# Attention and two MLPs on one core: the first attention unit worked in halves of three chunks

## Chip, cores and metric

The kernel runs on one core of one Trainium2 chip. The metric is the device time of one execution in microseconds (us).

## What is computed

Three stages follow one another. A gated linear attention makes `x`; a mixture of eight experts routes its 3072 rows by capacity and puts each through one expert; a gated MLP with RMS norm makes the output. The change touches the attention alone:

```python
B, H, S, D = q.shape                      # 4, 8, 768, 48
f = 1.0 / (1.0 + np.exp(-f_logit))
for t in range(S):
    state = f[:, :, t, :, None] * state + np.einsum('bhd,bhe->bhde', k[:, :, t], v[:, :, t])
    y[:, :, t] = np.einsum('bhd,bhde->bhe', q[:, :, t], state)
```

## The kernel before

**Attention** (`attention`, lines 323 to 539). The 32 heads are worked in 16 units of two heads, each head's 48 values of `d` on partitions 0 to 47 or 64 to 111, time along the free axis. A unit's 768 steps are six chunks of 128. One unit goes through these steps:

- `load` (line 348): SP's queue brings `f`, `k`, `q` (128x768, 384 KB each, laid out so on the host) and `v` (288 KB). There are three buffers of `f`, `k`, `q` and four of `v`; from unit 3 on each of the first comes as two transfers of 48 rows.
- `decays` (394): ACT makes `G`, the sigmoid of `f`, and `fs`, its first column of each chunk.
- `scans` (401): VectorE sets six columns of `G` (405), makes the running product `P` of the decays in each chunk by one scan over all 768 columns (406), takes six reciprocals (408), makes the inverse products `W` by a second scan from the back (409), and `kt` = k times W (418). GpSimd makes `qt` = q times P in two halves of 384 columns (414) and `e` (416).
- `k_back` (425): TensorE transposes five chunks of `kt`, three into one bank of PSUM and two into another, and ACT copies them to `kn` (432).
- `inner` (434): TensorE's products `kt` by `qt`, six chunks for two heads, in two groups of three chunks with a bank for each head (443); ACT copies a bank to `at` (449) and GpSimd masks it (450). The text calls these copies and masks.
- `sums` (452): TensorE's ten products `kn` by `v` into `U` (457), then VectorE's scan `st` over the chunks (461).
- `ends` (420): ACT keeps the last column of each chunk (`pall`) and `z`.
- `values` (464), two units later: TensorE makes `y` from `st`, `qt`, `at`, `v` (475), and ACT copies it to `YT` (481). After every fourth unit come the router's logits (`logits`, `logits_sum`).

The order is written out by hand: the scheduler is off, each engine has its instructions in the order of the program, and a unit `i` of the loop at line 509 issues `values(i-2)`, `k_back(i)`, `scans(i+1)`, `inner(i)`, `decays(i+2)`, `sums(i)`, `ends(i+1)`, then the loads of `f`, `k`, `q` for unit `i+4`:

```python
    for i in range(-1, NU + 2):
        ...
        if on(i):
            k_back(i)
        ...
        if on(i + 1):
            scans(i + 1)
        if i < 0:
            ends(0)
        if on(i):
            inner(i)
```

So unit 0 is scanned in the round `i = -1`, and its TensorE work lies in round 0, behind the instructions of unit 1's scans on VectorE and GpSimd. `bank()` hands out four banks of PSUM in turn. Ahead of the loop TensorE multiplies `ident` by itself eight times (502), without use of the result; this is called warm-up here. Two small loads are issued on ACT's queue ahead of the first sigmoid: `gcol` (720, the norm's weights, used in the last stage) and `wgp` (377, in two parts, the router's weights, used by the logits). A transfer signals one of eight completion counters; they are handed out in turn over SP's and ACT's transfers, and a transfer's issue waits until the one that had its counter before has landed.

**Behind attention.** The routing, then the experts and the gated MLP, are not touched.

Of the kernel before, what the change touches and what calls it, by code (L numbers as in the profile page):

```python
# [7 lines left out]
F32 = mybir.dt.float32  # L8
# [5 lines left out]
OP = mybir.AluOpType  # L14
# [308 lines left out]
def attention(tc, fT, kT, qT, vL, YT, w_gate, lg, pmin, ident, extra):  # L323
# [23 lines left out]
    def raw(nm, i):  # L347
        return RAW[nm, i % NR]
# [15 lines left out]
    load("fkq", 0)  # L364
# [11 lines left out]
    for h in range(2):  # L376
        nc.scalar.dma_start(wgp[64 * h:64 * h + D, :, 0:8], w_gate.rearrange("(p h d) e -> h d p e", h=2, d=D)[h])
# [15 lines left out]
    def decays(i):  # L393
        if not 0 <= i < NU:
            return
        G[i] = wk.tile([128, S + 1], F32, name="G")
        FS[i] = wk.tile([128, NC], F32, name="fs")
        nc.scalar.activation(G[i][:, 0:S], raw("f", i), AF.Sigmoid)
        nc.scalar.activation(FS[i], raw("f", i)[:, 0:S:C], AF.Sigmoid)

# [19 lines left out]
    def ends(i):  # L420
        if on(i):
            nc.scalar.copy(pall[:, i], P[i][:, C - 1:S:C])
            nc.scalar.copy(Z[i % 2][:, :, 1:], EZ[i][:, None, :].to_broadcast([128, D, NC - 1]))

    def k_back(i):
        KN[i] = wk.tile([128, NC, 128], F32, name="kn")
        for g, m in ((0, 3), (1, 2)):
            o = bank().rearrange("p (n c) -> p n c", n=3)
            for n in range(m):
                c0 = (3 * g + n) * C  # L430
                nc.tensor.transpose(o[:, n, :], KT[i][:, c0:c0 + C], ident)
            nc.scalar.copy(KN[i][:, 3 * g:3 * g + m], o[:, 0:m])

    def inner(i):

        AT[i] = wk.tile([128, 2, NC, C], F32, name="at", bufs=3)
        for g in range(2):
# [63 lines left out]
    for _ in range(8):  # L501
        nc.tensor.matmul(o, ident, ident, start=True, stop=True)
    decays(0)
    load("q", 1)
# [3 lines left out]
    for i in range(-1, NU + 2):  # L508
# [7 lines left out]
        if on(i):  # L516
            k_back(i)
        if i == NU - 1:
            extra["range"]()
        if on(i + 1):  # L520
            scans(i + 1)
        if i < 0:
            ends(0)
        if on(i):
            inner(i)
            decays(i + 2)
            sums(i)
            ends(i + 1)
# [161 lines left out]
def tile_kernel(ctx, tc, q, k, v, f_logit, w_gate, w1, w2, w2_gate, w2_val, w2_out, rms_g, fT, kT, qT, vL, out):  # L690
# [29 lines left out]
    nc.scalar.dma_start(gcol, rms_g.rearrange("(c p) -> p c", p=128))  # L720
# [21 lines left out]
    attention(tc, fT, kT, qT, vL, YT, w_gate, lg, pmin, ident,  # L742
# [460 lines left out]
```

## Time and profile before

| what | value |
|---|---|
| median of 3 runs | 836.42 us (835.05 to 838.92) |
| the profiled execution | 838.31 us, its span 836.6 us |
| TensorE busy | 804.6 us, 96% of the span |
| VectorE, ACT, GpSimd busy | 58%, 47%, 33% |
| mean granted clock of TensorE | 0.983 |
| warm-up products | 1.55 to 5.33 us |
| attention's sixteenth unit, first transposes | 105.56 us |

The span runs from the first to the last instruction. "Granted clock" is the share of TensorE's full clock that it was given: 1.00 is 2.4 GHz, 0.50 is 1.2 GHz. A row of the timeline gives the start, the time, the engine and line, what was written from what, and how many instructions were merged; in square brackets stands how long the engine was idle before it and what ended that. A 128x128 product in float32 shows as two instructions, a transpose as one. ACTq and SPq are the issue of transfers, not the transfers.

### The profile page before, as it was taken

How to read it: one execution, taken by the hardware profiler on the slowest of the kernel's cores; microseconds unless marked ns; L12 is line 12 of the kernel's file. 1: busy time of each engine (PE TensorE's matmuls, PEld its weight loads, DVE VectorE, ACT ScalarE, POOL GpSimd, SP SyncE). 2: the span in 40 equal slices, each digit the busy share in tenths (PEclk: the TensorE clock that was granted, in tenths of full speed). 3: DMA queues.
4: the chain of work that ended last, by engine and by line, in shares of the span. 5: the costliest groups of instructions: out<-in, count | busy, mean ns of one | idle time of the engine just before them, and what ended most of it. 6: DMA issues, size and time to landing. Idle time of an engine off the chain costs nothing.

```text
span 836.6 us, 16614 instructions
## 1 busy us (share of the span) xinstructions
PE 804.6 (96%) x6609; PEld 775.5 (93%) x6609; DVE 484.0 (58%) x868; ACT 392.0 (47%) x833; POOL 274.3 (33%) x327
## 2 busy tenths in 40 slices
PE   6999997899999999999999999999999999999996
PEld 5878876799999899999999999999999999999996
DVE  7988858488888888674443434344344434344332
ACT  5877636155555554576343443424243443424221
POOL 7877700348777677350112020110102020110100
PEclk8999998799999999999999999999999999999998
DMA  9986228487886697541000000000000000000000
GB/s 275 227 214 182 58 69 298 136 294 240 304 266 230 233 316 270 183 151 39 1 20 20 2 20 1 20 2 20 1 20 21 1 20 1 20 1 20 2 20 19
DMA packets 43684, 88.55 MB, mean 106 GB/s; under 512 B 5424, under 2 KB 22832, under 8 KB 43600
## 3 DMA queue, kind: packets, MB, share of 16 engines
q1 hardware_dynamic: 34528, 70.89, 27.0%
q0 software_dynamic: 3072, 9.44, 3.3%
q10 hardware_dynamic: 6000, 7.09, 2.4%
q8 instruction: 53, 0.87, 0.4%
q14 instruction: 31, 0.25, 0.1%
HBM read 70.89 MB, written 16.52 MB: 104 GB/s over the span
## 4 chain that ended last, share of the span: by engine, by line
PE 61%; issue 8%; DVE 8%; DMA 2%; ACT 2%; POOL 1%; ACTq 0%; DVEq 0%; POOLq 0%
PE o L572 5%; PE o L570 5%; PE o L571 5%; PE g L570 5%; PE g L572 5%; PE g L571 5%; PE v L572 5%; PE v L570 5%; PE v L571 5%; PE x L571 3%; PE x L572 2%; PE x L570 2%; DVE w L762 2%; PE h L571 2%; PE h L570 2%
## 5 line engine op out<-in xcount | busy, mean ns | idle before, releaser
L1127 DVE TENSOR_TENSOR hf<-sg,v 128x256 f32<-128x256 f32 x144 | 59.9, 416 | 165.3 <-PE v L572 115.1
L893 POOL TENSOR_TENSOR xlo<-xn,xhi 128x256 fp32r<-128x256 f32 x36 | 29.5, 823 | 312.2 <-ACT xhi L892 312.2
L1130 ACT CAST hh<-hf 128x256 fp32r<-128x256 f32 x144 | 58.6, 407 | 132.7 <-DVE hf L1127 132.7
L572 PE MATMUL g<-xhi,w 128*128 128x256 f32 x432 | 119.3, 276 | 0.0
L571 PE MATMUL g<-xlo,w 128*128 128x256 f32 x432 | 119.2, 276 | 0.0
L572 PE MATMUL v<-xhi,w 128*128 128x256 f32 x432 | 119.2, 276 | 0.0
L570 PE MATMUL v<-xhi,w 128*128 128x256 f32 x432 | 119.2, 276 | 0.0
L571 PE MATMUL v<-xlo,w 128*128 128x256 f32 x432 | 119.2, 276 | 0.0
L570 PE MATMUL g<-xhi,w 128*128 128x256 f32 x432 | 119.2, 276 | 0.0
L1131 DVE TENSOR_TENSOR hl<-hf,hh 128x256 fp32r<-128x256 f32 x144 | 61.3, 425 | 68.1 <-ACT hh L1130 68.1
L572 PE MATMUL o<-w,hl 128*128 128x384 f32 x288 | 98.6, 342 | 0.0
L570 PE MATMUL o<-w,hh 128*128 128x384 f32 x288 | 97.6, 339 | 0.2 <-ACT hh L1130 0.2
L571 PE MATMUL o<-w,hh 128*128 128x384 f32 x288 | 97.1, 337 | 0.0
L1125 ACT ACTIVATE sg<-g 128x256 f32<-128x256 f32 x144 | 55.3, 384 | 87.9 <-PE g L572 87.4
L570 PEld LDWEIGHTS g<-xhi,w 128*128 128x128 f32 x432 | 81.1, 188 | 0.0
L572 PEld LDWEIGHTS g<-xhi,w 128*128 128x128 f32 x432 | 81.1, 188 | 0.0
L570 PEld LDWEIGHTS v<-xhi,w 128*128 128x128 f32 x432 | 81.1, 188 | 0.0
L571 PEld LDWEIGHTS v<-xlo,w 128*128 128x128 f32 x432 | 81.1, 188 | 0.0
L572 PEld LDWEIGHTS v<-xhi,w 128*128 128x128 f32 x432 | 81.1, 188 | 0.0
L571 PEld LDWEIGHTS g<-xlo,w 128*128 128x128 f32 x432 | 81.0, 188 | 0.0
L958 POOL TENSOR_TENSOR nr<-nr,ne 128x384 f32<-128x384 f32 x36 | 61.4, 1707 | 45.7 <-DVE ne L957 12.5
L571 PE MATMUL x<-hl,w 128*128 128x384 f32 x192 | 65.6, 342 | 5.0 <-DVE hl L1032 4.8
(222 smaller groups left out, 1890.2 us busy)
## 6 DMA issues: line engine op xcount, KB each, us to landing
wraw<-in_moe_w_dram SPq DMA_DIRECT2D x32, 768.0 KB, 6.3
v<-in_v_rows_dram SPq DMA_DIRECT2D x16, 288.0 KB, 4.9
x_dram<-xrows SPq DMA_DIRECT2D x24, 192.0 KB, 4.8
nraw<-in_moe_w_gate_dram SPq DMA_DIRECT2D x12, 384.0 KB, 4.3
nraw<-in_moe_w_val_dram SPq DMA_DIRECT2D x12, 384.0 KB, 4.2
nraw<-in_moe_w_out_dram SPq DMA_DIRECT2D x12, 384.0 KB, 3.5
raw_f<-in_f_logit_turned_dram SPq DMA_DIRECT2D x26, 144.0 KB, 5.5
raw_k<-in_k_turned_dram SPq DMA_DIRECT2D x26, 144.0 KB, 5.0
```

Of the source, the lines that this page charges most:

```text
L570: nc.tensor.matmul(out, lhs[0], rhs[0], start=first, stop=False)
L571: nc.tensor.matmul(out, lhs[0], rhs[1], start=False, stop=False)
L572: nc.tensor.matmul(out, lhs[1], rhs[0], start=False, stop=last)
L762: eng.tensor_tensor(out=lo, in0=raw, in1=hi.bitcast(F32), op=OP.subtract)
L893: eng.tensor_tensor(out=lo, in0=s, in1=hi.bitcast(F32), op=OP.subtract)
L958: nc.gpsimd.tensor_tensor(out=r, in0=r, in1=e2.bitcast(F32), op=OP.mult)
L1125: nc.scalar.activation(sg, pg, AF.Silu)
L1127: nc.vector.tensor_tensor(out=h, in0=sg, in1=pv, op=OP.mult)
L1130: nc.scalar.copy(hh, h)
L1131: nc.vector.tensor_tensor(out=hl, in0=h, in1=hh.bitcast(F32), op=OP.subtract)
```

## The change

Unit 0 is worked in halves of three chunks (384 columns). Its `f` comes in two transfers; ACT's sigmoid is two instructions; VectorE does memset, scan, reciprocal, scan and `kt` for the first half and then for the second (`scans_half`). TensorE transposes and multiplies the first half (`k_back(0, (0,))`, `inner(0, (0,))`), then the second. All of this is now issued in round -1, ahead of unit 1's scans, with `ends(0)` behind it. The warm-up has 13 products instead of 8. The loads of `wgp` and `gcol` are issued behind the first sigmoids.

```diff
@@ -361,7 +361,10 @@
-    load("fkq", 0)
+    HF = (slice(0, S // 2), slice(S // 2, S))
+    for t in HF:
+        nc.sync.dma_start(raw("f", 0)[:, t], fT[0][:, t])
+    load("kq", 0)
     load("fk", 1)
...
@@ -373,8 +376,6 @@
-    for h in range(2):
-        nc.scalar.dma_start(wgp[64 * h:64 * h + D, :, 0:8], w_gate.rearrange("(p h d) e -> h d p e", h=2, d=D)[h])
...
@@ -395,8 +396,26 @@
-        nc.scalar.activation(G[i][:, 0:S], raw("f", i), AF.Sigmoid)
+        for t in HF if i == 0 else (slice(0, S),):
+            nc.scalar.activation(G[i][:, t], raw("f", i)[:, t], AF.Sigmoid)
         nc.scalar.activation(FS[i], raw("f", i)[:, 0:S:C], AF.Sigmoid)
+
+    def scans_half(t):
+        g, a, b = G[0], t.start, t.stop
+        if a == 0:
+            P[0], W[0], KT[0] = (wk.tile([128, S], F32, name=n) for n in ("P", "W", "kt"))
+            QT[0] = wk.tile([128, S], F32, name="qt", bufs=3)
+        nc.vector.memset(g[:, a + (C if a else 0):b:C], BIG * 1.0e8)
+        nc.vector.tensor_tensor_scan(out=P[0][:, t], data0=g[:, t], data1=one[:, t], initial=1.0, op0=OP.mult,
+                                     op1=OP.min)
+        nc.vector.reciprocal(g[:, a + C:b + 1:C], P[0][:, a + C - 1:b:C])
+        nc.vector.tensor_tensor_scan(out=W[0][:, t][:, ::-1], data0=g[:, b:a:-1], data1=one[:, t], initial=1.0,
+                                     op0=OP.mult, op1=OP.max)
+        nc.gpsimd.tensor_tensor(out=QT[0][:, t], in0=raw("q", 0)[:, t], in1=P[0][:, t], op=OP.mult)
+        if a:
+            EZ[0] = wk.tile([128, NC - 1], F32, name="e")
+            nc.gpsimd.tensor_tensor(out=EZ[0], in0=P[0][:, C - 1:S:C][:, 0:NC - 1], in1=FS[0][:, 1:], op=OP.mult)
+        nc.vector.tensor_tensor(out=KT[0][:, t], in0=raw("k", 0)[:, t], in1=W[0][:, t], op=OP.mult)
...
@@ -422,19 +441,22 @@
-    def k_back(i):
-        KN[i] = wk.tile([128, NC, 128], F32, name="kn")
-        for g, m in ((0, 3), (1, 2)):
+    def k_back(i, gs=(0, 1)):
+        if 0 in gs:
+            KN[i] = wk.tile([128, NC, 128], F32, name="kn")
+        for g in gs:
+            m = 3 - g
...
-    def inner(i):
+    def inner(i, gs=(0, 1)):
...
@@ -498,9 +520,12 @@
-    for _ in range(8):
+    for _ in range(13):
         nc.tensor.matmul(o, ident, ident, start=True, stop=True)
     decays(0)
+    for h in range(2):
+        nc.scalar.dma_start(wgp[64 * h:64 * h + D, :, 0:8], w_gate.rearrange("(p h d) e -> h d p e", h=2, d=D)[h])
+    nc.scalar.dma_start(gcol, rms_g.rearrange("(c p) -> p c", p=128))
     load("q", 1)
...
@@ -513,16 +538,22 @@
-        if on(i):
+        if i > 0 and on(i):
             k_back(i)
         if i == NU - 1:
             extra["range"]()
-        if on(i + 1):
+        if i < 0:
+            for t in HF:
+                scans_half(t)
+            for g in range(2):
+                k_back(0, (g,))
+                inner(0, (g,))
+            ends(0)
+        elif on(i + 1):
             scans(i + 1)
-        if i < 0:
-            ends(0)
         if on(i):
-            inner(i)
+            if i:
+                inner(i)
...
@@ -717,7 +748,6 @@
-    nc.scalar.dma_start(gcol, rms_g.rearrange("(c p) -> p c", p=128))
```

The orders that result, for the places that the prediction speaks of. `bank` and `U` are in PSUM; numbers behind `raw_` and `v_` tell buffers apart. First TensorE from its first instruction to unit 1's sums, before:

```order
L502 MATMUL bank<-ident 128x128 x8
L431 MATMUL bank<-ident,kt 128x128 x5
L443 MATMUL bank<-qt,kt 128x128 x12
L457 MATMUL U<-v_113,kn 48x48 x10
L431 MATMUL bank<-ident,kt 128x128 x5
L443 MATMUL bank<-qt,kt 128x128 x12
L457 MATMUL U<-v_114,kn 48x48 x10
```
and in the changed kernel:

```order
L524 MATMUL bank<-ident 128x128 x13
L452 MATMUL bank<-ident,kt 128x128 x3
L465 MATMUL bank<-qt,kt 128x128 x6
L452 MATMUL bank<-ident,kt 128x128 x2
L465 MATMUL bank<-qt,kt 128x128 x6
L479 MATMUL U<-v_112,kn 48x48 x10
L452 MATMUL bank<-ident,kt 128x128 x5
L465 MATMUL bank<-qt,kt 128x128 x12
L479 MATMUL U<-v_113,kn 48x48 x10
```
The six products of the first half now stand ahead of the second half's two transposes. GpSimd from its last constant on, before:

```order
L62 IOTA pid 128x1
L414 TENSOR_TENSOR qt<-raw_q_110,P 128x384 x2
L416 TENSOR_TENSOR e<-P,fs 128x5
L414 TENSOR_TENSOR qt<-raw_q_111,P 128x384 x2
L416 TENSOR_TENSOR e<-P,fs 128x5
L450 AFFINE_SELECT at<-at 128x384 x4
L414 TENSOR_TENSOR qt<-raw_q_112,P 128x384 x2
```
and now:

```order
L62 IOTA pid 128x1
L414 TENSOR_TENSOR qt<-raw_q_109,P 128x384 x2
L417 TENSOR_TENSOR e<-P,fs 128x5
L472 AFFINE_SELECT at<-at 128x384 x4
L433 TENSOR_TENSOR qt<-raw_q_110,P 128x384 x2
L435 TENSOR_TENSOR e<-P,fs 128x5
L433 TENSOR_TENSOR qt<-raw_q_111,P 128x384 x2
```
Unit 0's four masks moved from behind unit 1's `qt` to ahead of it. ACT from its first instruction on, before:

```order
L720 DMA gcol<-in_moe_rms_g_dram 128x3x1
L377 DMA wgp<-in_moe_w_gate_dram 48x4x8 x2
L398 ACT_TABLE_LOAD
L398 ACTIVATE G<-raw_f_104 128x768
L399 ACTIVATE fs<-raw_f_104 128x6
L398 ACTIVATE G<-raw_f_105 128x768
L399 ACTIVATE fs<-raw_f_105 128x6
L422 COPY pall<-P 128x6
L423 COPY z_137<-e 128x48x5
L432 COPY kn<-bank 128x384
L432 COPY kn<-bank 128x256
```
and now:

```order
L400 ACT_TABLE_LOAD
L400 ACTIVATE G<-raw_f_103 128x384 x2
L401 ACTIVATE fs<-raw_f_103 128x6
L527 DMA wgp<-in_moe_w_gate_dram 48x4x8 x2
L528 DMA gcol<-in_moe_rms_g_dram 128x3x1
L400 ACTIVATE G<-raw_f_104 128x768
L401 ACTIVATE fs<-raw_f_104 128x6
L453 COPY kn<-bank 128x384
L471 COPY at<-bank 128x384 x2
L453 COPY kn<-bank 128x256
L471 COPY at<-bank 128x384 x2
L441 COPY pall<-P 128x6
```
The table load comes first, the small loads stand between the sigmoids of units 0 and 1, and unit 0's copies stand ahead of `pall` and `z`. SP's queue from its fifth transfer on, with what each issue waits for (DMAHW0 to DMAHW7 are the completion counters), before:

```order
L359 DMA raw_k_108<-in_k_turned_dram 128x768
L359 DMA raw_q_111<-in_q_turned_dram 128x768 [waits DMAHW0_49]
L355 DMA v_113<-in_v_rows_dram 128x576 [waits DMAHW1_49]
L359 DMA raw_f_106<-in_f_logit_turned_dram 128x768 [waits DMAHW2_49]
L359 DMA raw_k_109<-in_k_turned_dram 128x768 [waits DMAHW3_49]
L359 DMA raw_q_112<-in_q_turned_dram 128x768 [waits DMAHW4_49]
L355 DMA v_114<-in_v_rows_dram 128x576 [waits DMAHW5_49]
L362 DMA raw_f_104<-in_f_logit_turned_dram 48x768 [waits DMAHW6_49,Activation_49]
```
and now:

```order
L359 DMA raw_k_107<-in_k_turned_dram 128x768
L359 DMA raw_q_110<-in_q_turned_dram 128x768 [waits DMAHW1_49]
L355 DMA v_112<-in_v_rows_dram 128x576 [waits DMAHW2_49]
L359 DMA raw_f_105<-in_f_logit_turned_dram 128x768 [waits DMAHW3_49]
L359 DMA raw_k_108<-in_k_turned_dram 128x768 [waits DMAHW4_49]
L359 DMA raw_q_111<-in_q_turned_dram 128x768 [waits DMAHW5_49]
L355 DMA v_113<-in_v_rows_dram 128x576 [waits DMAHW6_49]
L362 DMA raw_f_103<-in_f_logit_turned_dram 48x768 [waits DMAHW7_49,DMAHW0_49,Activation_49]
```
In the changed kernel the counters 5, 7 and 0 are those of `wgp` and `gcol`, so the third `q` and the fourth `f` wait for these.

## Rows read from the trace of the kernel before

**Rows 1.** Timeline of TensorE: start us, us, engine line op, tile, count.

```profile
22.12 0.77 PE L431 MATMUL bank<-ident,kt 128*128 128x128 f32 x5
...
22.82 1.68 PE L443 MATMUL bank<-qt,kt 48*128 48x128 f32 x24
...
25.01 1.42 PE L475 MATMUL yp<-qt,st 48*48 48x128 f32 x20
...
27.81 0.77 PE L431 MATMUL bank<-ident,kt 128*128 128x128 f32 x5
...
105.56 0.77 PE L431 MATMUL bank<-ident,kt 128*128 128x128 f32 x5
```

**Rows 2.** Same view, the first 17 us.

```profile
1.55 3.78 PE L502 MATMUL bank<-ident 128*128 128x128 f32 x16 [1.55 <-POOL ident L710]
...
10.60 1.33 PE L431 MATMUL bank<-ident,kt 128*128 128x128 f32 x5 [5.27 <-DVE G L405]
...
15.70 1.00 PE L431 MATMUL bank<-ident,kt 128*128 128x128 f32 x5
...
16.63 1.92 PE L443 MATMUL bank<-qt,kt 48*128 48x128 f32 x24
```

**Rows 3.** Timeline of VectorE, units 0 to 3.

```profile
5.34 0.06 DVE L405 MEMSET G<- 128x6 f32 x1 [1.86 <-ACT G L398]
...
9.24 1.31 DVE L418 TENSOR_TENSOR kt<-raw_k,W 128x768 f32<-128x768 f32 x1
...
10.50 0.06 DVE L405 MEMSET G<- 128x6 f32 x1
...
14.41 0.96 DVE L418 TENSOR_TENSOR kt<-raw_k,W 128x768 f32<-128x768 f32 x1
...
15.88 0.76 DVE L461 TENSOR_TENSOR_SCAN st<-U,z 128x288 f32<-128x288 f32 x1 [0.51 <-PE U L457]
...
16.77 1.75 DVE L406 TENSOR_TENSOR_SCAN P<-G,one 128x768 f32<-128x768 f32 x1
...
22.33 1.75 DVE L406 TENSOR_TENSOR_SCAN P<-G,one 128x768 f32<-128x768 f32 x1
```

**Rows 4.** Windows: us, busy by engine, PEclk (granted clock), DMA share, GB/s.

```profile
9.00:9.50 0.50, 0.00 (x0) 0.00 (x0) 0.47 (x2) 0.50 (x2) 0.50 (x1) 0.90 1.01 387
16.00:16.50 0.50, 0.50 (x5) 0.46 (x3) 0.50 (x1) 0.50 (x3) 0.50 (x2) 0.78 1.12 240
```

**Rows 5.** Timeline of SP's queue, ACT and GpSimd, the first 14 us.

```profile
0.82 0.40 SPq L359 DMA_DIRECT2D raw_f<-in_f_logit_turned_dram  x1
...
2.39 1.28 ACT L398 ACT_TABLE_LOAD   x1 [2.39 <-DVE wgp L375]
...
4.42 0.84 ACT L398 ACTIVATE G<-raw_f 128x768 f32<-128x768 f32 x1 [0.75 <-DMA raw_f<-in_f_logit_turned_dram]
...
7.79 1.95 POOL L414 TENSOR_TENSOR qt<-raw_q,P 128x384 f32<-128x384 f32 x2 [1.46 <-DMA raw_q<-in_q_turned_dram]
...
8.66 0.84 ACT L398 ACTIVATE G<-raw_f 128x768 f32<-128x768 f32 x1 [3.29 <-DMA raw_f<-in_f_logit_turned_dram]
...
12.44 1.96 POOL L414 TENSOR_TENSOR qt<-raw_q,P 128x384 f32<-128x384 f32 x2 [1.83 <-DVE P L406]
```

**Rows 6.** Windows of the first loads (columns as in rows 4).

```profile
2.00:3.00 1.00, 1.00 (x7) 1.00 (x7) 0.81 (x5) 0.61 (x1) 1.00 (x2) 1.00 0.95 270
3.00:4.00 1.00, 1.00 (x6) 1.00 (x6) 0.28 (x2) 0.67 (x1) 0.79 (x5) 1.00 0.69 124
```

**Rows 7.** Line 450 (masks): duration ns min/median/max, first and last start us.

```profile
L450 POOL TENSOR_SCALAR_AFFINE_SELECT at<-at x1: 1247/1247/1247, 14.5 to 14.5; 128x384 f32<-128x384 f32 x1
...
L450 POOL TENSOR_SCALAR_AFFINE_SELECT at<-at x2: 520/521/522, 16.2 to 16.7; 128x384 f32<-128x384 f32 x2
```

**Rows 8.** Timeline of SP's queue and ACT: f of unit 3.

```profile
9.41 0.83 SPq L362 DMA_DIRECT2D raw_f<-in_f_logit_turned_dram  x2
...
19.12 0.86 ACT L398 ACTIVATE G<-raw_f 128x768 f32<-128x768 f32 x1
```

More of the change, by code (lines that the diff above doesn't have):

```diff
@@ L320, in slots, with attention @@
         nc.vector.tensor_copy(ix[:, :, 2:3], t1[:, :, 2:3])
-def attention(tc, fT, kT, qT, vL, YT, w_gate, lg, pmin, ident, extra):
+def attention(tc, fT, kT, qT, vL, YT, w_gate, lg, pmin, ident, gcol, rms_g, extra):
     nc = tc.nc
@@ L432, in k_back @@
             nc.scalar.copy(KN[i][:, 3 * g:3 * g + m], o[:, 0:m])
-    def inner(i):
-        AT[i] = wk.tile([128, 2, NC, C], F32, name="at", bufs=3)
-        for g in range(2):
+    def inner(i, gs=(0, 1)):
+        if 0 in gs:
+            AT[i] = wk.tile([128, 2, NC, C], F32, name="at", bufs=3)
+        for g in gs:
             o = [bank().rearrange("p (n c) -> p n c", n=3) for _ in range(2)]
@@ L741, in tile_kernel @@
     ctx.enter_context(tc.manual_schedule())
-    attention(tc, fT, kT, qT, vL, YT, w_gate, lg, pmin, ident,
+    attention(tc, fT, kT, qT, vL, YT, w_gate, lg, pmin, ident, gcol, rms_g,
               {-2: consts, 1: lambda bank: turn_inc(tc, K, bank[:, 0:128], ident), "range": prepare,
```

## The prediction

> **What bounds the kernel now.** I read the timeline of TensorE first, because the page gives it the largest share. From the third unit on it begins each unit's transposes 5.69 us after the last ones, and the sixteenth unit's stand at 105.56 us [rows 1]. No pause lies between: TensorE works without a break from 10.60 us [rows 2] until the sixteenth unit, and what follows hangs on it (projections, then the routing, then the experts). So in attention the end is set by when TensorE starts unit 1 and how fast it gets through the first units. Two things can move that.
>
> The first is VectorE, which makes kt. Its timeline shows unit 0 beginning at 5.34 us, after the sigmoid of the whole f, unit 1 at 10.50, and the kt of unit 1 ending at 14.41 + 0.96 = 15.37 [rows 3]. TensorE takes that kt at 15.70 [rows 2], 0.33 late, because it is still at unit 0. The second is TensorE's clock. Unit 0 ran at the lower level (1.2 GHz): the granted clock goes from 1.00 to 0.50 within 9.0 to 9.5 us and comes back within 16.0 to 16.5 [rows 4]. The same 5 transposes, 12 products and 10 sums that take 2.89 us later (22.12 to 25.01 [rows 1]) took 15.70 - 10.60 = 5.10 us in unit 0 [rows 2].
>
> The profiled execution took 838.31 us, of which 836.6 are span; the median of the three runs is 836.42. The sum below is a difference, which I put against 838.31 (profile) and carry over to the median.
>
> **The first half of f (gain).** f is issued at 0.82 us, ACT takes it at 4.42 and VectorE starts at 5.34 [rows 3, 5]. The half has 0.197 MB. By the bytes of the windows, 0.197 MB have come by about 2.7 us and all 0.393 MB by about 4.0 [rows 6], so the half can land some 1.2 us sooner, near 3.2; at worst it lands no sooner than the whole. I take 3.4, near the early end: the small loads that stand beside f now (gcol, wgp) also go later, and the table load, which stands behind their issue and ends at 2.39 + 1.28 = 3.67 [rows 5], comes to the front. The sigmoid of 384 columns takes between half and all of the 0.84 us that 768 take [rows 5]; I take 0.52, near the half. VectorE then begins at 3.4 + 0.52 + 0.08 = 4.0, that is 1.34 us sooner. VectorE had been idle for 1.86 us before 5.34 [rows 3], so its own clearing of buffers, done by 3.5, does not hold this up.
>
> By the Trainium skill, page "DMA: Bandwidth & Descriptors", section "Anatomy of one DMA", a transfer has about 2.0 us that do not depend on its size, and only bytes / 436 GB/s that do. That speaks against halving: the estimate from it is 0.45 us saved where I take about 1.0, and the sum would be 0.55 us smaller. The row's whole f took 3.6 us from issue to use, which is longer than the 2.9 of that rule, so no row here decides it.
>
> **Two halves (loss).** A scan of 768 columns takes 1.75 us, one of 288 takes 0.76 [rows 3]; on that line 384 columns take 0.96. A half is then 0.09 (memset) + 1.00 + 0.23 (reciprocal) + 1.00 + 0.5 (half of a kt of 0.96), together 2.82, and two make 5.64, against 10.50 - 5.34 = 5.16 before. That 5.16 had a kt of 1.31 in it [rows 3], which ran beside the product q times P on GpSimd until 9.74 [rows 5]; the second half's kt can meet the same product, for 0 to 0.35 us. I add 0.15. Unit 0 ends at 4.0 + 5.8 = 9.8, against 10.50: gain 0.7. Unit 1's sigmoid must be done by then; it was at 8.66 + 0.84 = 9.50 [rows 5], and f of unit 1 stands no later by bytes.
>
> **What moves on GpSimd and ACT (loss).** In the new order the four masks of unit 0 stand ahead of unit 1's q times P on GpSimd, and ACT's copies for them stand behind the sigmoid of unit 1. Before, q times P ran at 12.44 to 14.40, and kt started at 14.41, just behind it [rows 3, 5]. Now the copies cannot begin before 9.5; with kn and four of 0.4 us, TensorE's second half between them, the last mask ends at about 13.0, and q times P runs at 13.0 to 15.0, over the kt of unit 1, due at about 13.8. The rows show what two such instructions do to each other: the kt of unit 0 took 1.31 us beside a product and that of unit 1 0.96 behind one [rows 3], and a mask took 1.25 us beside kt and 0.52 alone [rows 7]. The price is bounded by 0 (no meeting) and by the rest of both products, 1.1. I take 0.2: kt waits for the product in progress, not for the one queued after it.
>
> By the Trainium skill, page "SBUF — State Buffer", section "Who interferes with whom", the later of the two fully blocks until the first is done. The trace agrees: the mask of 1.25 us began at 14.50 beside a kt that ended at 15.37, and ended 0.38 after it.
>
> **TensorE (gain).** kt of unit 1 then ends at 15.37 - 0.7 + 0.2 = 14.87, and TensorE, done with unit 0 at about 12, takes it at once: the 0.33 us between 15.37 and 15.70 go. If its clock is high by then, the part of unit 1 that ran low goes too: 1.00 - 0.77 for the transposes and 1.92 - 1.68 for the products [rows 1, 2], 0.47 us. The 13 warm-up products, 26 instructions instead of 16 in 3.78 us [rows 2], add at most 2.36 us and end by 7.7; the first transposes have their kt at about 6.9, but the products after them wait for q times P (7.79 + 1.0 before [rows 5]), so that is covered; without that cover 0.7 us would show.
>
> **Costed at nothing.** Three small loads are issued on ACT's queue between the sigmoids; an issue takes about 0.4 us, and ACT was idle there for 3.29 us [rows 5]. SP's loads wait in turn for these to land: f of unit 3 was issued at 9.41, and its sigmoid ran at 19.12 [rows 8]. If it goes out 3 us later for that, its sigmoid can be 3 us late less what it had in hand, and VectorE needs it for the scan that stood at 22.33 [rows 3] and would now stand at 21.0: 21.0 - 19.98 leaves 1.0 us even if the load had nothing in hand before. Beyond that the lag would go straight to VectorE. q and v of unit 0 are one issue later, under 0.5 us, and v is needed only for unit 0's sums, which have 2.5 us before st. All later units keep their rows.
>
> **Sum.** -0.7 (unit 0 on VectorE) + 0.2 (port) - 0.33 (TensorE late no more) - 0.47 (clock) = -1.3 us. VectorE's next unit takes 5.56 us (16.77 to 22.33 [rows 3]), TensorE's 5.69, so TensorE stays the bound and hands the gain on to the end. The profile would come to 837.0, the median to **835.1 us**. That is 0.16%; about 0.5% (4.2 us) is what a measurement of this kernel can tell from no change.
>
> **Rivals.**
> *A, the clock falls in the new pause.* TensorE is done with unit 0 at about 12.0 and idle until 14.9. Before, it fell about 4.1 us after the last warm-up product ended (5.33 to about 9.45) [rows 2, 4]. If it falls before 14.9, unit 1 pays what unit 0 paid: 5.10 - 2.89 = 2.21 more instead of 0.47 less. The sum becomes -0.7 + 0.2 - 0.33 + 2.21 = +1.4: slower, 837.8. It decides if the granted clock is 0.50 when unit 1's transposes begin. Against: the pause is shorter than 4.1 us and the warm-up runs on to 7.7. For: between 7.7 and 12 TensorE is at work only about half the time.
> *B, the port is taken by both products.* If the second half of q times P goes first too, kt of unit 1 ends at 15.8, and -1.3 becomes -0.4: 836.0.
> *C, the change does not bring f sooner.* If the half lands when the whole did, VectorE starts 0.32 sooner, the halves cost 0.63, and of the gain only -0.33 - 0.47 + 0.3 + 0.2 = -0.3 stays: 836.1. A half that lands by the fixed share of the page gives -0.75.
> *D, SP's loads come too late*: f of unit 3 lands more than 1 us after the time that the sum allows; at 2 us more than that the gain is gone and +0.7 is left: 837.1.
>
> **Chances.** Forecast 0.45, A 0.30, B 0.12, C 0.08, D 0.05. The cases lie between -1.9 (half early, no port) and +1.4; the three runs shown spread over 3.9 us, so the median of another three can lie 1.5 off. This makes 833.2 to 838.4. All cases lie within 4.2 us, so chances beyond it are for what I have not seen, such as another phase of the clock in the routing: faster 0.04, same 0.93, slower 0.03.
>
> **What would show it.** VectorE's first scan at about 4.1 us and kt of unit 0 done in two parts by 9.8; unit 1's kt at 13.8, of 0.96 us or stretched (B); unit 1's transposes at about 14.9 at 0.15 us each; granted clock 1.00 from 7.7 on (A: 0.50 in 12 to 20); unit 2's transposes at 20.8 instead of 22.12, and then 5.69 us a unit. The forecast is wrong if unit 2's transposes stand at 22 or later, or if the difference at the sixteenth unit is not the one at the third.

## The result: slower by 0.6%, and the profile after

The changed kernel takes 842.96 us (median of 7 runs, 840.44 to 844.04), the kernel before 836.79 beside it (7 runs, 834.57 to 839.18): a ratio of 1.0061, 95% interval 1.0041 to 1.0081. For scale: the kernel before, run a second time against itself, gave 1.0020 (1.0000 to 1.0039). I had forecast 835.1 and a range up to 838.4; the time is 8 us over the forecast and outside the range. The profiled execution took 842.96 us, span 841.3, mean granted clock 0.976 (before: 838.31, 836.6, 0.983).

TensorE's timeline of the changed kernel, where [rows 1, 2] stood before: start us, us, engine, line, operation, count, and in brackets the idle time ahead and what ended it. L524 is the warm-up, L452 transposes, L465 products, L479 sums, L497 values.

```profile
1.54 4.95 PE L524 MATMUL bank<-ident 128*128 128x128 f32 x26 [1.54 <-POOL ident L741]
6.81 0.55 PE L452 MATMUL bank<-ident,kt 128*128 128x128 f32 x3 [0.32 <-DVE G L408]
8.26 0.94 PE L465 MATMUL bank<-qt,kt 48*128 48x128 f32 x12 [0.90 <-POOL qt L414]
9.73 0.41 PE L452 MATMUL bank<-ident,kt 128*128 128x128 f32 x2 [0.54 <-DVE G L424]
...
11.26 0.66 PE L479 MATMUL U<-v,kn 128*48 128x48 f32 x20 [0.25 <-DMA v<-in_v_rows_dram]
14.55 0.74 PE L452 MATMUL bank<-ident,kt 128*128 128x128 f32 x5 [2.64 <-DVE kt L437]
15.22 2.98 PE L465 MATMUL bank<-qt,kt 48*128 48x128 f32 x24
...
19.51 2.41 PE L497 MATMUL yp<-qt,st 48*48 48x128 f32 x20
21.85 2.80 PE L497 MATMUL yp<-at,v 128*48 128x128 f32 x24
24.58 1.33 PE L452 MATMUL bank<-ident,kt 128*128 128x128 f32 x5
...
30.77 0.77 PE L452 MATMUL bank<-ident,kt 128*128 128x128 f32 x5
```

Up to 14.55 us all goes as planned or better: unit 0 is worked in two pieces from 6.81, and unit 1's transposes start 1.15 us sooner than the 15.70 of before. Then unit 1's 12 products (24 instructions) take 2.98 us instead of 1.92 [rows 2] and the values behind them 2.41 + 2.80, at the lower level from 15.55 us on, and unit 2 begins at 24.58 instead of 22.12 [rows 1]. The windows show the granted clock (third column from the right):

```profile
15.50:16.00 0.50, 0.50 (x10) 0.50 (x10) 0.50 (x1) 0.50 (x2) 0.00 (x0) 0.55 1.00 195
25.50:26.00 0.50, 0.50 (x4) 0.17 (x5) 0.07 (x1) 0.48 (x2) 0.00 (x0) 0.71 0.93 258
```

It falls within 15.5 to 16.0 us and is back within 25.5 to 26.0. Before, it had fallen within 9.0 to 9.5 and come back within 16.0 to 16.5 [rows 4], so that unit 0 paid, ahead of unit 1's kt, and unit 1 hardly. Now unit 0 is fast, in time that TensorE spends waiting anyway, and unit 1, which all later units follow, is slow. The same 5 transposes, 12 products, sums and values that lead from unit 1 to unit 2 take 10.03 us instead of 6.42 (15.70 to 22.12).

VectorE's timeline, against [rows 3]:

```profile
3.93 0.95 DVE L409 TENSOR_TENSOR_SCAN P<-G,one 128x384 f32<-128x384 f32 x1
...
6.20 0.56 DVE L418 TENSOR_TENSOR kt<-raw_k,W 128x384 f32<-128x384 f32 x1
...
9.64 1.75 DVE L425 TENSOR_TENSOR_SCAN P<-G,one 128x768 f32<-128x768 f32 x1
...
13.45 0.96 DVE L437 TENSOR_TENSOR kt<-raw_k,W 128x768 f32<-128x768 f32 x1
...
28.15 0.76 DVE L483 TENSOR_TENSOR_SCAN st<-U,z 128x288 f32<-128x288 f32 x1 [2.58 <-ACT at L471]
```

First scan at 3.93, unit 1's first scan at 9.64 (memset 9.54 against 10.50), its kt at 13.45 in 0.96 us: VectorE has gained 0.96 us. At 28.15 it has waited 2.58 us: the profile names ACT's copy, and the sums of unit 2, which `st` reads, end on TensorE at 27.38 + 0.66 = 28.04. So the gain arrives at VectorE and ends at that wait.

From unit 3 on each unit takes 5.69 us again, but for those with router logits. The sixteenth stands at 107.79 us (105.56 before), and the transposes of the rows behind attention at 120.54 (118.32 before). The difference of the spans is 4.7 us, so 2.2 of it arose in attention and 2.5 behind it, where the clock is low for 27.3 us of 138 to 173 (17.1 us of 135 to 160 before). The second part is less than executions of the changed kernel differ by there (716.3 to 720.8 us behind attention, below), and a third profile of the kernel before is at the lower level for 23.9 us there.

### The profile page after: what moved, and what is told of

It reads as the page before. It is cut to its first block, busy times and chain, and to the rows that moved or that the text cites. A ratio compares the mean times of both kernels' runs of the same rounds, so it can differ in the third digit from the quotient of the medians.

```text
span 841.3 us, 16643 instructions
## 1 busy us (share of the span) xinstructions
PE 811.3 (96%) x6619; PEld 780.7 (93%) x6619; DVE 485.1 (58%) x873; ACT 392.2 (47%) x834; POOL 273.9 (33%) x327
## 4 chain that ended last, share of the span: by engine, by line
PE 63%; issue 8%; DVE 7%; ACT 2%; DMA 1%; POOL 1%; ACTq 0%; DVEq 0%; POOLq 0%
PE o L603 5%; PE o L601 5%; PE o L602 5%; PE g L601 5%; PE g L602 5%; PE g L603 5%; PE v L603 5%; PE v L602 5%; PE v L601 5%; PE x L602 3%; PE x L603 3%; PE h L602 3%; PE h L601 3%; PE x L601 3%; PE h L603 3%
## 5 line engine op out<-in xcount | busy, mean ns | idle before, releaser
L601 PE MATMUL h<-xhi,w 128*128 128x384 f32 (+2 forms) x198 | 68.8, 347 | 0.7 <-ACT xhi L1093 0.6
```

Of the source, the lines that this page charges most:

```text
L601: nc.tensor.matmul(out, lhs[0], rhs[0], start=first, stop=False)
```

## The experiments

A fill, below, is a 128x128 product of the identity whose result nobody reads, so that the output stays the same. "Unit 1 to 2" is the time from unit 1's first transpose to unit 2's, "idle" TensorE's wait ahead of unit 1's, "end" the start of the rows' transposes behind attention, "behind" the span less that. Ratios are to the kernel before, run beside each (its medians there: 836.12 to 837.36 us). "Fall" is a change of the granted clock from 1.00 to 0.50. What two sets of the same kernel differ by, 0.2% in before_again, is the scale for the ratios near 1.

| kernel | idle | unit 1 to 2 | unit 2 | end | behind | median us | ratio, 95% interval |
|---|---|---|---|---|---|---|---|
| before | 0 | 6.42 | 22.12 | 118.32 | 718.3 | 836.79 | |
| before_again | 0 | 6.42 | 21.88 | 117.33 | 716.9 | 837.14 | 1.0020 (1.0000 to 1.0039) |
| before_3 (one run) | 0.35 | 6.39 | 21.97 | 118.07 | 718.5 | 838.35 | |
| changed | 2.64 | 10.03 | 24.58 | 120.54 | 720.8 | 842.96 | 1.0061 (1.0041 to 1.0081) |
| after_again | 1.61 | 10.97 | 26.93 | 122.40 | 718.2 | 842.07 | 1.0080 (1.0053 to 1.0108) |
| after_3 (one run) | 1.88 | 7.52 | 22.62 | 118.03 | 716.3 | 836.04 | |
| after_4 (one run) | 2.38 | 10.32 | 25.16 | 120.56 | 716.8 | 839.14 | |
| fill_pause | 0 | 5.84 | 22.36 | 117.75 | 716.4 | 835.94 | 1.0008 (0.9985 to 1.0031) |
| front_fills | 3.49 | 9.97 | 25.90 | 121.76 | 714.5 | 839.17 | 1.0017 (1.0004 to 1.0030) |
| early_fills | 0 | 6.50 | 21.23 | 116.63 | 715.8 | 834.57 | 0.9978 (0.9966 to 0.9990) |
| te_late | 1.04 | 10.11 | 24.95 | 120.39 | 718.6 | 840.70 | 1.0049 (1.0026 to 1.0071) |
| warm8 | 1.55 | 10.61 | 25.26 | 120.67 | 715.6 | 838.54 | 1.0025 (1.0009 to 1.0040) |
| whole_fills | 0 | 5.86 | 21.24 | 117.50 | 718.0 | 834.79 | 0.9978 (0.9957 to 0.9998) |
| before_fills | 0.25 | 5.87 | 21.41 | 117.72 | 716.2 | 834.08 | 0.9965 (0.9950 to 0.9980) |
| before_warm | 1.15 | 5.87 | 21.39 | 117.73 | 716.3 | 837.13 | 0.9999 (0.9980 to 1.0017) |
| before_warm2 | 1.17 | 5.87 | 21.33 | 116.79 | 716.6 | 835.42 | 0.9988 (0.9969 to 1.0006) |
| loads_back | 1.23 | 5.87 | 21.69 | 117.90 | 714.9 | 834.83 | 0.9973 (0.9958 to 0.9989) |
| loads_only | 0.25 | 5.87 | 20.88 | 116.43 | 715.0 | 834.60 | 0.9966 (0.9947 to 0.9985) |
| loads_plain | 0 | 6.52 | 21.50 | 116.95 | 717.9 | 836.23 | 0.9987 (0.9970 to 1.0003) |
| delay_late | 0 | 6.85 | 22.46 | 119.48 | 718.0 | 836.45 | 1.0010 (0.9993 to 1.0027) |

**The two kernels again** (before_again and after_again, no edit).

> The changed kernel, unchanged, for a second profile. Theory 'pause': the granted clock falls to 0.50 between 12 and 16 us again and unit 2's transposes stand near 24.6, the sixteenth unit's near 107.8. Rival 'chance': the fall is missing in this execution and unit 2's transposes stand near 20.8. Time 840 to 844 us.

> The kernel before, unchanged, for a second profile. If the clock's changes come at fixed times of the program, its fall near 9.4 us and its rise near 16.2 stand where they stood, and the sixteenth unit's transposes at 105.6; if they come at other times in each execution, the rise and with it the sixteenth unit move by up to about 1.5 us. Time 834 to 839 us.

The loss is there again, 1.0080, and in this execution attention loses still more: the clock falls at 10.06, earlier than I expected (12 to 16), unit 1 waits less, but stays slow to the end.

```profile
15.96 1.30 PE L452 MATMUL bank<-ident,kt 128*128 128x128 f32 x5 [1.61 <-DVE kt L437]
...
26.93 0.84 PE L452 MATMUL bank<-ident,kt 128*128 128x128 f32 x5
```

**Fill the pause** (fill_pause), behind the sums of unit 0:

```diff
             sums(i)
+            if i == 0:
+                o = bank()[:, 0:128]
+                for _ in range(10):
+                    nc.tensor.matmul(o, ident, ident, start=True, stop=True)
```

> The changed kernel with ten products of ident by itself (20 instructions, about 2.4 us at the higher clock) behind unit 0's sums, in the pause before unit 1's transposes. Theory 'pause': the clock stays at 1.00 from the warm-up on, unit 2's transposes come at 20.5 to 21, the sixteenth unit's at about 104.3 instead of 107.8, and the time is at least 3 us below the changed kernel's; if the loss behind attention has its own cause, 839 us, if it hangs on the attention's end, 835.5. Rival 'halves': the halves themselves cost the time, the fill changes nothing, 843 us.

TensorE's timeline of fill_pause (L562 the fills):

```profile
13.31 3.37 PE L562 MATMUL bank<-ident 128*128 128x128 f32 x20
16.52 0.71 PE L452 MATMUL bank<-ident,kt 128*128 128x128 f32 x5
...
22.36 0.77 PE L452 MATMUL bank<-ident,kt 128*128 128x128 f32 x5
```

Unit 1 starts 2 us later than in the changed kernel, partly because q came late in this execution (unit 0's first products at 9.62) and the fills, slow at first, lasted until then; unit 2 still stands 2.2 us sooner. The clock did fall, at 11.75, which I had not expected, but was back at 15.16, ahead of unit 1. The loss of 6 us is gone in the median: 835.94 us where after_again, run beside it, has 842.07, though its twelve runs spread from 832.61 to 843.27. So it is the clock, and it is decided ahead of unit 1; the halves in themselves do no harm that this time shows. One thing is not separated in the halves' order: `bank()` in the fill also moves the turn of the four banks by one. In the order of before the clock stays up with that (before_fills) and without it (before_warm).

**A later end of attention alone** (delay_late): the kernel before with nine fills ahead of the last unit's values.

> The kernel before with nine products of ident ahead of the last unit's values, a delay of 2.2 us at the end of attention and nothing else. Theory 'later stages': a later end of attention by itself moves the routing and the first expert against the clock's changes and costs about 4 us more, 841 to 843 us. Rival 'no more than the delay': 839 us, and the half-clock time behind 130 us stays near 24 us.

The fills take 2.27 us and put the rows' transposes 1.56 us later (14.32 us behind the sixteenth unit's transposes, 12.76 before). The ratio is 1.0010 (0.9993 to 1.0027), so a later end by itself costs at most 2.3 us, itself included: theory 'later stages' (841 to 843 us) falls. The rival's 839 us did not come either.

**Which idle stretch?** front_fills fills the waits between the halves (one more warm-up product, four fills ahead of the first half's products, two ahead of the second half's transposes) and leaves the pause; early_fills fills both (as front_fills, and eleven behind the sums).

> early_fills without the eleven throw-away products behind unit 0's sums: the waits between the halves are filled, the wait of about 2.6 us ahead of unit 1 is left. If the long pause alone costs the clock: a fall at 14 to 18 us, unit 2's transposes at 24 to 27, 840 to 843 us. If the waits between the halves cost it: no fall, unit 2 at 21.0 to 21.4, 834 to 835.5 us. If it takes both: now one and now the other, a median between 835 and 840 and a spread over 5 us.

> The changed kernel with throw-away 128x128 products of the identity in every wait of TensorE between the warm-up and unit 1: 14 warm-up products, four ahead of the first half's products, two ahead of the second half's transposes, eleven behind unit 0's sums. Theory 'pause' (the halves do bring VectorE and unit 1 forward by about 1 us, and the sparse start and the pause of 2.6 us behind it lose the clock): the clock shows no fall before unit 2, unit 1's transposes start at 14.5 to 15.0, unit 2's at about 20.8, the sixteenth at about 104, and the time is 834 to 836 us, level with or up to 2 us under the kernel before. Theory 'no gain' (the halves bring nothing to the end even at full clock, since something else sets unit 2): unit 2 at 22 or later and 836 to 837 us. Theory 'chance' (the clock behind attention decides): no prediction for unit 2, and a time that follows the microseconds at half clock in the whole run.

TensorE in front_fills (L454 transposes, L469 products, L483 sums):

```profile
11.79 0.66 PE L483 MATMUL U<-v,kn 128*48 128x48 f32 x20 [0.32 <-DMA v<-in_v_rows_dram]
15.93 0.74 PE L454 MATMUL bank<-ident,kt 128*128 128x128 f32 x5 [3.49 <-DVE kt L437]
16.60 2.92 PE L469 MATMUL bank<-qt,kt 48*128 48x128 f32 x24
...
25.90 1.23 PE L454 MATMUL bank<-ident,kt 128*128 128x128 f32 x5
```

With work up to 12.4 us and then a pause of 3.49, the clock falls at 16.66 and is back at 26.90: for the loss in attention the pause alone is enough. But the time is 839.17 us, only 0.17% over the kernel before, although attention ends at 121.76, later than in the changed kernel (120.54). So the pause alone does not make the whole 0.6%. With both filled the clock shows no fall before 126 us, the durations are those of the higher level, and the time is 834.57 us, 0.2% under the kernel before.

**Order and warm-up.** te_late keeps the halves on VectorE, ACT and the loads and puts TensorE's and GpSimd's part of unit 0 back behind unit 1's scans; warm8 is the changed kernel with 8 warm-up products.

```diff
-        if i > 0 and on(i):
+        if on(i):
             k_back(i)
...
-            for g in range(2):
-                k_back(0, (g,))
-                inner(0, (g,))
             ends(0)
...
-            if i:
-                inner(i)
+            inner(i)
```

> The changed kernel with f, the scans and the products with q and k of unit 0 still in halves, but TensorE's and GpSimd's part of unit 0 put back where the kernel before has it: its transposes, products and masks as a whole unit in the round behind unit 1's scans. Theory 'pause': unit 0 starts at about 10 us instead of 6.8 and 9.7, its work runs closer up to unit 1's, the wait ahead of unit 1 shrinks from 2.6 us to under 1, VectorE keeps its 1 us, and the time comes back to 835 to 837 us. Theory 'halves' (the halves themselves, by the stretched product with q or by what they change behind, cost the time): it stays at 841 to 843 us.

> The changed kernel with the eight warm-up products of the kernel before instead of thirteen, so that TensorE waits 1.6 us longer ahead of the first half's transposes. Theory 'pause': the busy share ahead of unit 1 falls further, so the clock is lost too, at the same place or earlier, and the time is 840 to 844 us; if the fall comes early enough that the clock is back by unit 1, as in the kernel before, the time is 836 to 838 us instead. If the five added products were what costs the clock, it would be back at 836 us with no fall ahead of unit 1.

TensorE in te_late, and then in warm8:

```profile
7.25 0.55 PE L452 MATMUL bank<-ident,kt 128*128 128x128 f32 x3
9.93 0.44 PE L452 MATMUL bank<-ident,kt 128*128 128x128 f32 x2 [2.13 <-DVE G L424]
...
14.84 1.30 PE L452 MATMUL bank<-ident,kt 128*128 128x128 f32 x5 [1.04 <-DVE kt L437]
...
24.95 0.76 PE L452 MATMUL bank<-ident,kt 128*128 128x128 f32 x5
```

```profile
6.87 0.90 PE L452 MATMUL bank<-ident,kt 128*128 128x128 f32 x3 [1.55 <-DVE G L408]
...
14.65 1.30 PE L452 MATMUL bank<-ident,kt 128*128 128x128 f32 x5 [1.55 <-DVE kt L437]
15.88 3.36 PE L465 MATMUL bank<-qt,kt 48*128 48x128 f32 x24
...
25.26 0.76 PE L452 MATMUL bank<-ident,kt 128*128 128x128 f32 x5
```

My expectation for te_late was a miss: the pause ahead of unit 1 shrank to 1.04 us, but the three early transposes and the wait of 2.13 behind them are left, the clock fell at 10.77 and came back only at 24.42. In warm8 unit 0 runs slowly (0.90 us for three transposes, 0.55 in the changed kernel) and nothing is fast until about 25 us; its time, 838.54, is under the 840 to 844 expected. TensorE is slow there from its first product on: 16 instructions in 3.78 us, 236 ns each, against 124 ns for the fills of early_fills (22 in 2.72 us). So no row shows whether warm8 lost the clock or had not got it yet.

```profile
1.55 3.78 PE L524 MATMUL bank<-ident 128*128 128x128 f32 x16 [1.55 <-POOL ident L741]
```

```profile
12.02 2.72 PE L566 MATMUL bank<-ident 128*128 128x128 f32 x22
```

Neither kernel has the pause of 2.6 us; both have little work for TensorE from 5 to 15 us, and unit 1 is slow in both. before_warm (31 warm-up products, up to 11.7 us) and loads_back waited 1.15 and 1.23 us ahead of unit 1, behind work with no gap over 0.5 us, and kept the clock.

> The kernel before with 31 warm-up products instead of 8 and nothing else. Theory 'sparse start' (the long stretch of little work ahead of unit 0 costs the clock, and a wait of 2 us behind a full stretch does not): the clock shows no fall ahead of unit 2, unit 1's transposes at 15.4 to 15.6 and 0.74 us, unit 2's at 21.4, the time 834 to 835.5 us as with before_fills. Theory 'pause' in its narrow form (any wait of 2 us ahead of unit 1 costs the clock): a fall at about 15 to 18 us, unit 2 at 23 to 25, the time 838 us or more.

> before_warm once more (the kernel before with 31 warm-up products), for a second profile. If its median of 837.1 us comes from executions in which the wait of about 1 to 2 us between unit 0's sums and unit 1's transposes costs the clock, this profile shows either no fall with unit 2 at 21.4 and 834 to 836 us, or a fall at 14 to 18 us, unit 2 at 23 to 25, and 837 us or more. If it shows no fall and 837 us or more, the loss lies behind attention.

Both profiles of before_warm show no fall in attention, but its two medians, 837.13 and 835.42, don't follow: between 834 and 840 us its executions differ in something that neither profile caught.

**What do the halves bring at full clock?** before_fills is the kernel before with 31 warm-up products and seven fills behind unit 0's sums; loads_only is that with the three small loads moved as in the change, without halves; loads_back is early_fills with those loads put back; loads_plain is the kernel before with the loads moved, no fill. whole_fills is te_late with 14 warm-up products and nine fills at each of two places.

> The kernel before, whole units and its own order, with the same kind of throw-away products: 31 in the warm-up instead of 8, so that they reach from 1.55 to about 10.5 us, and seven behind unit 0's sums. It is the fair rival of early_fills: both hold the clock, only the halves differ. Theory 'pause' with a gain of the halves: unit 0's transposes 0.7 us instead of 1.33, unit 1's at about 15.4, when VectorE hands over its product with k (15.37 before), unit 2's at about 21.5, and 835 to 836.5 us, so early_fills is ahead of it by 0.5 to 1 us. If the clock in itself were worth what the halves bring, it would be level with early_fills.

> before_fills with those three small loads moved behind unit 0's sigmoid, as the change has it, f, scans and TensorE's order whole. If the small loads delay f (its packets or the table load), the sigmoid of the whole f starts at 3.9 to 4.4 instead of 4.79 us, VectorE's first scan at 4.9 to 5.3 instead of 5.80, and all of it passes to unit 1 and 2 (unit 2's transposes at 20.7 to 21.2 instead of 21.41), time 833.3 to 834.1 us; if not, 4.8 us and 834.1 us as before_fills.

> early_fills with the three small loads of ScalarE's queue (the gate's two and the one of the norm) put back ahead of the table load, as in the kernel before; f still comes in halves. It splits the first term of the sum (VectorE starts 1.34 us sooner by the plan): if the halving of f alone brings it, the first sigmoid stays at 3.3 to 3.5 us and VectorE's first scan at 4.0; if the small loads were the larger part, the table load is at about 2.4 again and ends at 3.7, the first sigmoid starts at 3.7 to 4.2, the first scan at 4.3 to 4.8, unit 2 up to 0.2 us later than in early_fills. The time: 834 to 835.5 us.

> te_late (f, scans and products with k and q of unit 0 in halves, TensorE's and GpSimd's part of unit 0 whole, behind unit 1's scans) with throw-away products: 14 in the warm-up, nine between the two groups of transposes of unit 0, nine behind its sums. Theory 'GpSimd's order' (in early_fills the halves' 0.8 us reach unit 2 as 0.18 only, because unit 0's masks stand ahead of unit 1's product with q, which is done at 15.45 instead of 14.42): unit 1's product with q done by 13.8, unit 1's products without a wait, unit 2's transposes at 20.6 to 20.8 instead of 21.23, the sixteenth at 103.2 to 103.5, the time 833 to 834.5 us. If something else holds unit 1 (its copies, TensorE's own sum of work), unit 2 stays at 21.1 or later.

> The kernel before with the three small loads behind unit 0's sigmoid and nothing else: no halves, no added product. VectorE starts at 5.0 to 5.1 us instead of 5.34 to 5.7, unit 0's transposes at 10.0 instead of 10.4 to 10.6 at half clock as before; with the clock back ahead of unit 1's products the time is 835.5 to 836.8 us, 0 to 0.7 us under the kernel before; if the earlier start moves the place where the clock comes back past unit 2, it is 838 us or more.

TensorE's unit 1 and 2 in before_fills, then early_fills, then loads_only:

```profile
15.54 0.74 PE L431 MATMUL bank<-ident,kt 128*128 128x128 f32 x5 [0.25 <-DVE kt L418]
16.20 1.63 PE L443 MATMUL bank<-qt,kt 48*128 48x128 f32 x24
...
21.41 0.77 PE L431 MATMUL bank<-ident,kt 128*128 128x128 f32 x5
```

```profile
14.73 0.74 PE L454 MATMUL bank<-ident,kt 128*128 128x128 f32 x5
15.40 0.94 PE L469 MATMUL bank<-qt,kt 48*128 48x128 f32 x12
16.55 1.11 PE L469 MATMUL bank<-qt,kt 48*128 48x128 f32 x12 [0.21 <-ACT kn L455]
...
21.23 0.76 PE L454 MATMUL bank<-ident,kt 128*128 128x128 f32 x5
```

```profile
15.01 0.74 PE L429 MATMUL bank<-ident,kt 128*128 128x128 f32 x5 [0.25 <-DVE kt L416]
15.67 1.63 PE L441 MATMUL bank<-qt,kt 48*128 48x128 f32 x24
...
20.88 0.77 PE L429 MATMUL bank<-ident,kt 128*128 128x128 f32 x5
```

The halves with the loads moved start unit 1 0.81 us sooner (14.73 against 15.54) and unit 2 only 0.18. Unit 1's second half of products has to wait (16.55), because q times P of unit 1 is late on GpSimd, behind unit 0's masks, and stretched beside kt:

```profile
11.72 0.99 POOL L476 TENSOR_SCALAR_AFFINE_SELECT at<-at 128x384 f32<-128x384 f32 x2 [0.48 <-ACT at L475]
12.69 2.76 POOL L433 TENSOR_TENSOR qt<-raw_q,P 128x384 f32<-128x384 f32 x2
```

```profile
15.63 0.39 ACT L442 COPY z<-e 128x240 f32<-128x240 f32 x1 [1.94 <-POOL e L435]
15.93 0.74 ACT L455 COPY kn<-bank 128x384 f32<-128x384 f32 x2
```

It ends at 15.45 instead of 14.42 in before_fills. The wait goes by way of ACT: e comes behind q times P on GpSimd, ACT's z waits 1.94 us for e, and behind z stands the copy kn, which TensorE's second half waits for. The small loads alone, with whole scans, bring unit 2 0.53 us forward (20.88) and the end of attention to 116.43, no later than with the halves (116.63); 0.76 of the 1.29 us that the end gains are the first logits, which are told of below. Like against like, the halves put unit 2 later: 21.23 against 20.88 with the loads moved, 21.69 (loads_back) against 21.41 with the loads in their old place. As times, 834.08, 834.57, 834.60, 834.79 and 834.83 us can't be told apart. whole_fills takes the masks out of the way and its unit 1 runs without that wait (5.86 us to unit 2 instead of 6.50), but in that execution k and q of unit 0 landed late (VectorE waited 0.39 us for k, and the second half's kt took 0.98 us instead of 0.56 beside q times P), so unit 2 stands at 21.24 and not at 20.7: the order is shown, the gain is not. The best that was run is the kernel before with fills, or with fills and the loads moved: both some 0.35% under it. loads_plain, the loads moved without a fill, can't be told from the kernel before (0.9987).

**Does the change lengthen what is behind attention?** Two more profiles of the changed kernel and one of the kernel before.

> The changed kernel a third time, for its profile. Theory 'pause': the fall ahead of or in unit 1 is there again, unit 2's transposes at 24 to 27 us, the transposes of the rows (attention's end) at 120.4 to 122.5. Behind attention, span less the start of those transposes: if the change itself lengthens it, 718 to 721 us again as in its two profiles; if executions differ, anything from 714.5 to 721.

> The same once more: unit 2's transposes at 24 to 27 us, attention's end at 120.4 to 122.5; behind it 718 to 721 us if the change lengthens it, 714.5 to 721 if executions differ.

> The kernel before a third time: a fall at 8.5 to 9.5, back at 15.4 to 16.3, unit 2's transposes at 21.8 to 22.2, attention's end at 117.3 to 118.4, and behind it 716.5 to 718.5 us as in its two profiles, or anything from 714.5 to 721 if executions differ.

No: behind attention the four profiles of the changed kernel took 720.8, 718.2, 716.3 and 716.8 us, the three of the kernel before 718.3, 716.9 and 718.5; of 125 to 200 us they spend 27.3, 20.5, 20.5 and 20.5 us at the lower level, and 17.1, 17.1 and 23.9. In attention the changed kernel varies from execution to execution, 118.03 to 122.40 at its end, as the fall stands at 11.88 (back at 18.70), 11.20 (24.85), 15.55 (25.79) or 10.06 us (27.12).

## Why the prediction was wrong, step by step

- **The first half of f: right, a little low.** VectorE's first scan stood at 3.93 (4.1 forecast). loads_back tells the two causes apart: with halves and the loads where they were, the first scan is at 4.37, against 5.80 in before_fills, so the halves bring 1.43 us; the loads bring 0.32 to 0.44 on top (4.05 in early_fills, 3.93 in the changed kernel), since without them the table load runs from 0.82 and not from 2.39. The page "DMA: Bandwidth & Descriptors" of the Trainium skill, section "Anatomy of one DMA", has a fixed 2.0 us and bytes at 436 GB/s; it states them for transfers that GpSimd issues, and f comes by SP's queue. The estimate from it is 2.45 us for the half; from issue (0.82) to the sigmoid (3.25) it took 2.43, and up to 2.58 in the other profiles of the changed kernel. For the whole f the estimate is 2.9, and loads_only took 3.30 (0.82 to 4.12), before_fills 3.97 beside the small loads. So halving saved more than the 0.45 us of that estimate, because the whole f took longer than it says.
- **The halves: right.** Unit 0 ended at 9.54 against 9.8 forecast, a gain of 0.96 against 0.7: it began 1.50 us sooner instead of 1.34, and working in halves cost 0.54 instead of 0.64.
- **The port: right in kind, priced on one side only.** In the changed kernel GpSimd's q times P of unit 1 stretched to 2.72 us from 1.96 and kt kept its 0.96; in front_fills and loads_back it was the other way, kt took 1.81. By the page "SBUF — State Buffer" of the Trainium skill, section "Who interferes with whom", the later one is blocked until the first is done; the rows of loads_back agree (kt from 13.86, q times P from 12.90 to 14.86, and 0.81 us left after that). For kt the price, 0 or 0.85 us by execution, lies in the bounds of 0 to 1.1; rival B did not set the time. The prediction priced nothing for a late q times P: in early_fills, at full clock, that cost TensorE, by way of ACT's z and kn, 0.63 us between units 1 and 2 (6.50 against 5.87). C and D did not happen: the half came sooner, and unit 3's scan began without a wait.

VectorE's unit 1 in loads_back:

```profile
4.37 0.95 DVE L411 TENSOR_TENSOR_SCAN P<-G,one 128x384 f32<-128x384 f32 x1
...
13.86 1.81 DVE L439 TENSOR_TENSOR kt<-raw_k,W 128x768 f32<-128x768 f32 x1
```

- **TensorE late no more: right.** Unit 1's transposes at 14.55 (14.87 forecast).
- **The clock, "-0.47": this is the step that failed.** It took for granted that the clock is high in unit 1 once unit 0 is. The lower level cost 3.61 us between unit 1 and 2 (10.03 against 6.42) and 0.50 in unit 2. By rows: -1.15 (unit 1's start) + 3.61 + 0.50 = +2.96 at unit 3; less 0.74, since the unit with the first logits took 9.34 us in the profiled execution of before and 8.60 in the changed kernel, makes +2.22, the 2.23 of the sixteenth unit. The prediction had no term for those 0.74 us: it read TensorE as without a break from 10.60 us on, but in the kernel before it waited for ACT at the logits:

```profile
44.88 0.93 PE L495 MATMUL bank<-ident,lgT 128*128 128x128 f32 x6 [1.30 <-ACT lgT L490]
```

- **Rival A was the mechanism, but mis-sized and mis-placed.** I gave it a chance of 0.30, +1.4 us and a test: the clock at 0.50 when unit 1's transposes begin. At 14.55 it was still 1.00; the fall came at 15.55, after the pause, in the middle of unit 1's products, and then lasted over unit 1's products, sums and values. I had priced only what unit 0 had paid before, transposes, products and sums (2.21), and nothing of the values and unit 2. The argument against A, a pause shorter than the 4.1 us after which the clock fell before, was the wrong reading: front_fills lost it after 3.49 us and the changed kernel after thin work and 2.64. Nor do the rows give the 4.1 us a start: the column reads 1.00 up to 9.0 us, but the warm-up of the kernel before ran at 236 ns an instruction (16 in 3.78 us [rows 2]), that is at the lower level, so when the clock rose isn't known. The upper end of the range, 838.4, also left little room for A: A's 837.8 and the 1.5 us of spread make 839.3.
- **What stays open.** The medians are 6 us apart, the profiled executions 2.6 on average (840.1 of four against 837.5 of three). The timed runs of the changed kernel have a mean granted clock of 0.971 to 0.978, median 0.976, the 29 of the kernel before run beside after_again 0.976 to 0.990, median 0.983: (1 - 0.976) x 2 x 841 = 40 us at the lower level against 28, an estimate. Half of those 12 us would be the 6 us lost, but the 28 can be short by some 7 us, since the record can miss the fall of the first units (before_3, in the last section). That the loss goes with the clock ahead of unit 1 is shown by fill_pause, which takes it back beside after_again, and early_fills agrees. How it divides over attention and the stages behind in the unprofiled executions is not shown: the profiled loss in attention is 2.2 us, and front_fills and warm8, which end attention 3.4 and 2.4 us later than the profile of before, are only 0.17 and 0.25% slower than the kernel before.

## What to carry to other kernels

An engine that gets its first work sooner, in pieces, can lose more by its clock than the start gains: ask not only when the first piece begins, but how dense the work is up to the point that everything later follows, and price a low clock over all the work that it may cover, not over the piece that paid last time. Where idle time near the start can't be avoided, throw-away products in it are a cheap test, and here they brought the time back, and 0.2 to 0.35% under the kernel before in five kernels, little more than the 0.2% that two sets of the same kernel differed by. And test the parts of a change alone: with the clock held, three small loads moved out of the way of f brought unit 2 forward by 0.53 us, and the halves did not bring it forward at all.

## Not expected of the hardware

- The clock can fall after the idle time and not in it: at 15.55 us in the changed kernel and at 16.66 in front_fills, when TensorE had been at work again for 1.0 and 0.7 us, and it was back only at 25.79 and 26.90, although hardly a gap lay between. In the kernel before it fell within the idle time (9.0 to 9.5 us, of 5.33 to 10.60 [rows 2, 4]).
- The granted clock's record starts at 1.00 whatever the clock: in warm8 no window up to 134 us shows less than 1.00, while five transposes took 1.30 us as at 0.50; in before_3 no window of attention does, while unit 0's five took 1.33. At the start durations must be read, not the column.
- The unit with the first logits took 9.34 us in the kernel before, 9.45 in before_fills and 9.40 in loads_back, and 8.60 in the changed kernel and early_fills. In before_fills ACT's copy of e waits for GpSimd; in early_fills, where GpSimd's q times P of that unit stands 0.8 us sooner (39.68 against 40.49), it doesn't. That VectorE's smaller lead is the cause is argued, not shown. ACT's timeline of before_fills (line 423), and of early_fills (line 442):

```profile
43.45 0.39 ACT L423 COPY z<-e 128x240 f32<-128x240 f32 x1 [0.76 <-POOL e L416]
```

```profile
42.34 0.42 ACT L442 COPY z<-e 128x240 f32<-128x240 f32 x1
```
